# Routed attention with a gated convolution FFN: slots of a head pair and half a batch's queries, the first batch's heads prepared up front, FFN by half batches

## The chip, the cores and the metric

One core of one Trainium2 chip runs the kernel. The metric is device microseconds for one execution of the whole program, the median of several runs. TensorE (PE in the profile) multiplies matrices and transposes, PEld is its weight load, VectorE is DVE, ScalarE is ACT, GpSimd is POOL, and SyncE (SP) issues most DMAs. Each engine takes its instructions in the order in which the program lists them and waits, at each, for the semaphores that it needs. PSUM has eight banks, all of which this kernel uses.

## The reference, cut to what matters

Four batches, eight heads, 768 tokens, head size 64; the FFN takes d_model 512 to d_ff 1024 and back, with a convolution of three taps along the sequence that makes the gate.

```python
q_assign = argmax(einsum(q_n, c_n))          # 16 clusters per head
k_assign = argmax(einsum(k_n, c_n))
mask = q_assign[:, :, :, None] == k_assign[:, :, None, :]
scores = where(mask, (q @ k.T) / 8, -1e9)
attn = softmax(scores); x = attn @ v         # heads side by side: 4 x 768 x 512

h = maximum(x @ w_in, 0.0)                   # 4 x 768 x 1024
conv = sum over k of conv_w[k] * h shifted by k - 1 along the sequence
out = (h * sigmoid(conv)) @ w_out
```

The mask never appears as a matrix. Every token carries extra rows in the score product, which depend on its cluster number and make the score of two tokens of different clusters so low that its exponential is zero.

## The kernel before

Tokens lie in the order "(p j)": partition p holds tokens 6p to 6p+5. Work is laid out by hand in program order, as a loop over 32 heads (four batches of eight), one head in each turn; a turn is called a slot here. It has six score steps, and each computes 128 keys against all 768 queries in two matmuls of 384 columns (`scores`, L174) into one of two PSUM pairs, which ScalarE exponentiates (L181, 128x768).

Between the score steps of slot t, other heads' and other batches' work is put:

- preparation of head t+2: six transposes of q and k side by side into the banks `tra` and `trb` (L104), their copy by VectorE (L108) and ScalarE (L109), the cast on GpSimd (L114) and two DMAs that carry the halves to `extq` and `extk` (L115, L116), the cast of v (L119), twelve small matmuls against the centroids (`assign`, L123), and the argmax: two VectorE operations (L136, L137), a product on GpSimd (L140), a reduction on VectorE (L149), three small GpSimd operations that make `pack` (L151 to L155). In the next slot `pack` is transposed (L158), copied (L162), and two DMAs carry the bias rows (L163, L164);
- the values of head t-1: 36 matmuls of 65 columns (L188) into the bank `avb`, then normalization (L201, L202), and for each second head the transposes of the pair's output (L212) and the copy to `xT` (L215);
- from slot 9 on, one FFN unit, which is a block of 128 features for all 768 tokens of a batch: four matmuls for each half of the tokens into the bank `fp` (`ffn_in`, L229), relu (L239), two copies on GpSimd that fill the shifted ends (`pads`, L243, L244), three taps on VectorE (L255, L257), tanh (L264) and gate (L276) in the slot after;
- output blocks (128 tokens, eight matmuls over the features, L288), also in `fp`, copied by VectorE (L302) and stored. They can start when all eight units of a batch are gated: slots 17 to 22 and 25 to 30.

SyncE's queue has the loads of q, k and v of head t+4 (L94 to L96), the two DMAs of the cast, the bias rows' DMAs and the stores, in program order. GpSimd also sets constant rows of `extq` and `extk` (`ext_rows`, L308 to L310) at the start and in slots 0 and 1, and issues the weights' DMAs.

Ahead of the loop, heads 0 and 1 are prepared. Behind it the last unit of batch 2, the whole FFN of batch 3 (eight units, `last_in`, `last_gate`, `last_out`) and twelve output blocks are left. There the first tap is ScalarE's (L253) and the gate comes from the sigmoid (L268, L282).

Of the kernel before, what the change touches and what calls it, by code (L numbers as in the profile page):

```python
# [17 lines left out]
def kernel(  # L18
# [15 lines left out]


# [11 lines left out]
    VW = D + 2  # L47

# [5 lines left out]

# [5 lines left out]
    avp = avb[:, 0 : J * VW].rearrange("p (j w) -> p j w", j=J)  # L60
    tra16 = tra.bitcast(F16)
    pkT = trb.bitcast(F16)[0 : 4 * J, 1024 - P : 1024]
    asn = trb[:, 256:448].rearrange("p (j t c) -> p j t c", j=J, t=2)
# [3 lines left out]
    xT = const.tile([P, B, R, S], F16, name="xT")  # L67
# [7 lines left out]
    kscale = const.tile([P, 2, J], F16, name="kscale")  # L75

    NE = 4
    extq_b = [const.tile([P, S], F16, name=f"extq{i}") for i in range(NE)]  # L80
    extk_b = [const.tile([P, S], F16, name=f"extk{i}") for i in range(NE)]
    v16_b = [const.tile([P, J, VW], F16, name=f"v16_{i}") for i in range(NE)]
    NHP = 3
    hpad_b = [const.tile([P, J + 2, P], F16, name=f"hpad{i}") for i in range(NHP)]

    def tok(t, hh):
        return t[hh // H, hh % H].rearrange("(p j) d -> p j d", j=J)
# [3 lines left out]
    def load(hh, kq=nc.sync):  # L91
        qk_t[hh] = rot.tile([P, J, 2, D], F32, name="qk_in", tag="qk_in", bufs=4)
        v_t[hh] = rot.tile([P, J, D], F32, name="v_in", tag="v_in", bufs=4)
        nc.sync.dma_start(qk_t[hh][:, :, 0], tok(q, hh))  # L94
        kq.dma_start(qk_t[hh][:, :, 1], tok(k, hh))
        nc.sync.dma_start(v_t[hh][:], tok(v, hh))  # L96


    qkT, c16, attn, x16, hg_b, packs, asgs = {}, {}, {}, {}, {}, {}, {}

    def transposes(h):
        for j in range(J):
            to = tra[:, P * j : P * (j + 1)] if j < 4 else trb[:, P * (j - 4) : P * (j - 3)]
            nc.tensor.transpose(to, qk_t[h][:, j].rearrange("p a d -> p (a d)"), id128[:])  # L104

    def qkT_copy(h):
        qkT[h] = rot.tile([P, S], F32, name="qkT", tag="qkT", bufs=2)
        nc.vector.tensor_copy(out=qkT[h][:, 0:512], in_=tra[:])  # L108
        nc.scalar.activation(qkT[h][:, 512:S], trb[:, 0:256], AF.Copy)  # L109
        del qk_t[h]  # L110

    def cast_qk(h):
        c = rot.tile([P, S], F16, name="c16", tag="c16", bufs=2)
        nc.gpsimd.tensor_copy(out=c[:], in_=qkT[h][:])  # L114
        nc.sync.dma_start(extq_b[h % NE][64:128, :], c[0:64, :])  # L115
        nc.sync.dma_start(extk_b[h % NE][64:128, :], c[64:128, :])  # L116

    def cast_v(h):
        nc.gpsimd.tensor_copy(out=v16_b[h % NE][:, :, 0:D], in_=v_t.pop(h)[:])  # L119

    def assign(h):
        for j in range(J):
            nc.tensor.matmul(  # L123
                trb[:, 256 + 32 * j : 288 + 32 * j],
# [6 lines left out]
    def arg_a(h):  # L131
# [3 lines left out]
        asgs[h] = val  # L135
        nc.vector.tensor_reduce(out=mx[:], in_=asn, axis=AX.X, op=ALU.max)  # L136
        nc.vector.tensor_tensor(  # L137
            out=eqq[:], in0=asn, in1=mx[:].unsqueeze(3).to_broadcast((P, J, 2, C)), op=ALU.is_equal
        )
        nc.gpsimd.tensor_tensor(  # L140
# [3 lines left out]
    def arg_b(h):  # L144
        m_t = rot.tile([P, J, 2], F32, name="m_t", tag="m_t")
        pack = rot.tile([P, 4, J], F16, name="pack", tag="pack")
        packs[h] = pack
        del qkT[h]
        nc.vector.tensor_reduce(out=m_t[:], in_=asgs.pop(h)[:], axis=AX.X, op=ALU.max)  # L149

        nc.gpsimd.tensor_scalar(  # L151
            out=pack[:, 1:3, :], in0=m_t.rearrange("p j t -> p t j"), scalar1=-8.5, scalar2=None, op0=ALU.add
        )
        nc.gpsimd.tensor_tensor(out=pack[:, 0:4:3, :], in0=pack[:, 1:3, :], in1=pack[:, 1:3, :], op=ALU.mult)
        nc.gpsimd.tensor_tensor(out=pack[:, 2:4, :], in0=pack[:, 2:4, :], in1=kscale[:], op=ALU.mult)  # L155

    def pack_transpose(h):
        nc.tensor.transpose(pkT, packs.pop(h).rearrange("p a j -> p (a j)"), id16[:])  # L158

    def bias_rows(h):  # L160
        spk = rot.tile([P, P], F16, name="spk", tag="spk")
        nc.vector.tensor_copy(out=spk[0 : 4 * J, :], in_=pkT)  # L162
        nc.sync.dma_start(extq_b[h % NE][0:2, :], spk[0 : 2 * J, :])  # L163
        nc.sync.dma_start(extk_b[h % NE][1:3, :], spk[2 * J : 4 * J, :])  # L164
# [3 lines left out]
    def scores(h, kt):  # L168
        if kt == 0:
            attn[h] = rot.tile([P, J, S], F16, name="attn", tag="attn", bufs=2)  # L170
        s = sc[nsc[0] % 2]
        nsc[0] += 1
        for half in range(2):
            nc.tensor.matmul(  # L174
                s[:, half, 0:HS],
                lhsT=extk_b[h % NE][:, P * kt : P * (kt + 1)],
                rhs=extq_b[h % NE][:, HS * half : HS * (half + 1)],
# [3 lines left out]
        nc.scalar.activation(  # L181
            attn[h][:, kt, :].rearrange("p (a c) -> p a c", a=2), s[:, :, 0:HS], AF.Exp, scale=0.125
        )

    def values(h, jqs):
        for jq in jqs:
            for kt in range(J):
                nc.tensor.matmul(  # L188
                    avp[:, jq, 0 : D + 1],
                    lhsT=attn[h][:, kt, P * jq : P * (jq + 1)],  # L190
                    rhs=v16_b[h % NE][:, kt, 0 : D + 1],
# [5 lines left out]
    def normalize(h):  # L197
        rec = rot.tile([P, J, 1], F32, name="rec", tag="rec")
        if h % 2 == 0:
            x16[h // 2] = rot.tile([P, J, P], F16, name="x16", tag="x16")  # L200
        nc.vector.reciprocal(out=rec[:], in_=avp[:, :, D : D + 1])  # L201
        nc.vector.tensor_tensor(  # L202
            out=x16[h // 2][:, :, D * (h % 2) : D * (h % 2 + 1)],
            in0=avp[:, :, 0:D],
# [189 lines left out]
    for t in range(NH):  # L394
# [9 lines left out]
        if t + 4 < NH:  # L404
            load(t + 4)
# [135 lines left out]
```

## Time and profile before

| what | us |
|---|---|
| median of 3 runs | 337.9 (337.27 to 339.41) |
| the profiled execution's span | 337.4 |
| first scores of slot 0 / 5 / 9 / 26 | 18.48 / 63.54 / 90.29 / 231.86 |
| end of the last score step | 280.81 |
| VectorE busy | 206.0 (61%) |
| ScalarE busy | 224.5 (67%) |
| GpSimd busy | 139.1 (41%) |
| exponentials: 192 of 0.81 | 151.6 |
| multiply-add taps: 64 of 1.03 | 65.9 |
| `extq`/`extk` constant rows: 12 of 0.73 | 8.7 |

The span is that of one profiled execution. A group's row gives the number of instructions, their busy time and mean duration, and the idle time of the engine ahead of them with the one that ended it. Matmuls overlap in TensorE's pipeline, so that the time from one start to the next, not the duration, tells what a matmul costs its queue. TensorE's granted clock (PEclk) is 1.00 at full speed.

### The profile page before, as it was taken

To read this page: it belongs to the slowest core of one execution; us is meant where nothing else is said; L and a number is where in the kernel's file an instruction comes from. 1 tells how busy PE (TensorE), PEld (TensorE's weight loads), DVE (VectorE), ACT (ScalarE), POOL (GpSimd) and SP (SyncE) were. 2 spreads that over 40 slices of the span, in tenths; PEclk is the share of its full clock that TensorE was granted. 3 is DMA by queue.
4 is the path that set the end of the run, shared out by engine and by line. 5 is a ranking of instruction groups with operands and counts; after the bars stand their busy time and mean duration, and the time that the engine had idled before them with its cause. 6 is when DMAs were issued, how large, how long until landed. Compare 5 with 4: busy or idle time off the path is not lost.

```text
span 337.4 us, 7211 instructions
## 1 busy us (share of the span) xinstructions
PE 283.8 (84%) x2721; PEld 198.4 (59%) x2721; DVE 206.0 (61%) x390; ACT 224.5 (67%) x339; POOL 139.1 (41%) x304
## 2 busy tenths in 40 slices
PE   7585969687989898989999999899999987699762
PEld 7463747566666666667666666666667654345320
DVE  3212424343467776868777778678878668646632
ACT  2143838567777787878777777787777785855532
POOL 3366464445544545455535454545454301110200
PEclk9855989999999999999999999999999999999877
DMA  7138475666733333434244444542431100021005
GB/s 199 39 96 190 104 130 141 130 159 139 182 98 96 94 97 96 105 94 111 75 132 119 126 115 123 142 104 74 129 101 55 58 33 1 31 95 62 0 0 187
DMA packets 66744, 34.26 MB, mean 102 GB/s; under 512 B 53395, under 2 KB 63635, under 8 KB 66710
## 3 DMA queue, kind: packets, MB, share of 16 engines
q1 hardware_dynamic: 63622, 31.51, 34.2%
q0 software_dynamic: 2304, 2.10, 4.3%
q8 instruction: 21, 0.34, 0.5%
q10 hardware_dynamic: 784, 0.20, 0.3%
q14 instruction: 13, 0.11, 0.1%
HBM read 23.11 MB, written 6.29 MB: 87 GB/s over the span
## 4 chain that ended last, share of the span: by engine, by line
PE 53%; ACT 23%; issue 8%; DVE 5%; POOL 5%; DMA 3%; SPq 2%; ACTq 0%; POOLq 0%; DVEq 0%
ACT attn L181 14%; PE trb L123 11%; PE sc L174 11%; PE fp L229 7%; PE avb L188 6%; PE fp L288 6%; PE sc L288 4%; ACT th L264 3%; ACT hpad L239 3%; ACT qkT L109 2%; PE sc L327 2%; DVE cnv L257 2%; PE tra L212 1%; DMA extk<-spk 1%; PE avb L229 1%
## 5 line engine op out<-in xcount | busy, mean ns | idle before, releaser
L181 ACT ACTIVATE attn<-sc 128x768 f16<-128x768 f32 x192 | 151.6, 810 | 72.9 <-PE sc L174 72.5
L174 PE MATMUL sc<-extq,extk 128*128 128x384 f16 x384 | 93.2, 334 | 24.1 <-ACT attn L181 11.6
L257 DVE SCALAR_TENSOR_TENSOR cnv<-hpad,cwcol,cnv 128x768 f16<-128x768 f16 x64 | 65.9, 1031 | 14.8 <-ACT cnv L253 12.9
L140 POOL TENSOR_TENSOR val<-eqq,iota_rev 128x192 f32<-128x192 f32 x32 | 26.6, 830 | 73.5 <-DVE eqq L137 73.5
L174 PEld LDWEIGHTS <-extk 128*128 128x128 f16 x384 | 30.8, 103 | 39.8 <-issue 16.0
L188 PE MATMUL avb<-v,attn 128*128 128x65 f16 x1152 | 53.3, 196 | 0.1
L188 PEld LDWEIGHTS <-attn 128*128 128x128 f16 x1152 | 47.6, 99 | 7.6 <-issue 0.3
L123 PEld LDWEIGHTS trb<-cT,qkT 128*128 128x128 f32 x384 | 48.8, 198 | 3.2 <-ACT qkT L109 1.0
L123 PE MATMUL trb<-cT,qkT 128*128 128x32 f32 x384 | 47.5, 275 | 0.8 <-DVE qkT L108 0.8
L229 PE MATMUL fp<-xT,w_in 128*128 128x384 f16 x224 | 46.2, 329 | 2.0 <-ACT hpad L239 0.7
L229 PEld LDWEIGHTS <-w_in 128*128 128x128 f16 x256 | 25.1, 99 | 26.4 <-issue 11.3
L243 POOL COPY hpad<-hpad 128x127 f16<-128x127 f16 x32 | 10.2, 319 | 66.9 <-ACT hpad L239 66.9
L288 PEld LDWEIGHTS <-hg 128*128 128x128 f16 x192 | 19.3, 101 | 29.3 <-DVE hg L282 6.2
L276 DVE SCALAR_TENSOR_TENSOR hg<-th,hpad 128x768 f16<-128x768 f32 x24 | 28.2, 1173 | 10.5 <-ACT th L264 10.4
L108 DVE COPY qkT<-tra 128x512 f32<-128x512 f32 x32 | 21.8, 682 | 18.5 <-PE tra L104 18.5
L114 POOL CAST c<-qkT 128x768 f16<-128x768 f32 x32 | 26.4, 825 | 14.8 <-DVE qkT L108 8.7
L239 ACT ACTIVATE hpad<-fp 128x384 f16<-128x384 f32 x56 | 27.6, 493 | 2.9 <-PE fp L229 1.8
L201 DVE RECIPROCAL rec<-avb 128x6 f32<-128x6 f32 x32 | 6.3, 196 | 34.6 <-PE avb L188 34.6
L119 POOL CAST v<-v_in 128x384 f16<-128x384 f32 x32 | 27.1, 848 | 0.0
L288 PE MATMUL fp<-w_out,hg 128*128 128x512 f16 x96 | 24.6, 379 | 0.0
L288 PE MATMUL sc<-w_out,hg 128*128 128x512 f16 x64 | 17.7, 413 | 7.2 <-DVE hg L282 5.3
L264 ACT ACTIVATE th<-cnv 128x768 f32<-128x768 f16 x24 | 20.3, 845 | 4.0 <-DVE cnv L257 4.0
(71 smaller groups left out, 303.4 us busy)
## 6 DMA issues: line engine op xcount, KB each, us to landing
qk_in<-in_q_dram SPq DMA_DIRECT2D x32, 192.0 KB
v_in<-in_v_dram SPq DMA_DIRECT2D x32, 192.0 KB
out_dram<-o_sb SPq DMA_DIRECT2D x24, 256.0 KB
qk_in<-in_k_dram SPq DMA_DIRECT2D x31, 192.0 KB
extq<-c SPq DMA_DIRECT2D x32, 96.0 KB
extk<-c SPq DMA_DIRECT2D x32, 96.0 KB
w_in<-in_moe_w_in_dram POOLq DMA_DIRECT2D x8, 128.0 KB, 4.2
w_out<-in_moe_w_out_dram POOLq DMA_DIRECT2D x8, 128.0 KB, 4.5
```

The lines of the kernel that those rows point to most:

```text
L119: nc.gpsimd.tensor_copy(out=v16_b[h % NE][:, :, 0:D], in_=v_t.pop(h)[:])
L123: nc.tensor.matmul(trb[:, 256 + 32 * j : 288 + 32 * j], lhsT=qkT[h][:, P * j : P * (j + 1)], rhs=cT32[:, h % H, :], start=True, stop=True,)
L140: nc.gpsimd.tensor_tensor(out=val[:], in0=eqq[:], in1=iota_rev[:].unsqueeze(1).unsqueeze(1).to_broadcast((P, J, 2, C)), op=ALU.mult)
L174: nc.tensor.matmul(s[:, half, 0:HS], lhsT=extk_b[h % NE][:, P * kt : P * (kt + 1)], rhs=extq_b[h % NE][:, HS * half : HS * (half + 1)], st ...
L181: nc.scalar.activation(attn[h][:, kt, :].rearrange("p (a c) -> p a c", a=2), s[:, :, 0:HS], AF.Exp, scale=0.125)
L188: nc.tensor.matmul(avp[:, jq, 0 : D + 1], lhsT=attn[h][:, kt, P * jq : P * (jq + 1)], rhs=v16_b[h % NE][:, kt, 0 : D + 1], start=(kt == 0) ...
L229: nc.tensor.matmul(bank[:, 0:HS], lhsT=w_in16[:, r, fb, :], rhs=xT[:, b, r, HS * half : HS * (half + 1)], start=(r == 0), stop=(r == R - 1 ...
L239: nc.scalar.activation(flat(hpad(b, fb)[:, 1 + 3 * half : 4 + 3 * half, :]), bank[:, 0:HS], AF.Relu)
L257: nc.vector.scalar_tensor_tensor(out=cnv[:], in0=src, scalar=w, in1=cnv[:], op0=ALU.mult, op1=ALU.add)
L264: nc.scalar.activation(th_t[b, fb][:], cnv_t.pop((b, fb))[:], AF.Tanh, scale=0.5)
L276: nc.vector.scalar_tensor_tensor(out=hg(b, fb), in0=th_t.pop((b, fb))[:], scalar=1.0, in1=flat(hpad(b, fb)[:, 1 : J + 1, :]), op0=ALU.add, ...
L288: nc.tensor.matmul(bank[:, 0:Dm], lhsT=hg_b[b][:, fb, P * sb : P * (sb + 1)], rhs=w_out16[:, fb, :], start=(fb == 0), stop=(fb == NFB - 1) ...
```

## The change

A slot is now a pair of heads with half of a batch's queries: slots 8b to 8b+3 take the four pairs of batch b for the first 384 queries, 8b+4 to 8b+7 for the other 384. There are 32 slots as before. A score step takes two blocks of 128 keys against 384 queries, so that its matmuls and its exponential have the old sizes. Queries are in sequence order; keys and values keep the order "(p j)". `extq` and `extk` have 67 rows instead of 128, without constant filler rows (the constant rows come with `pack`), and there are twelve of each instead of four.

Preparation of a head is done earlier and kept: heads 0 to 2 are begun ahead of the loop, heads 3 to 5 stand in slot 0, heads 6 and 7 in slot 1, and head h in slot h-6 from head 8 on. For heads 0 and 1 the argmax is VectorE's alone. Loads of q and k are eight heads ahead in the loop, over six buffers instead of four.

An FFN unit is two feature blocks for half of a batch's tokens: the first half gates tokens 0 to 381, the second half the other 386, and a small copy on GpSimd (`carry`) hands three columns from one to the other in place of `pads`. A half can start when its four slots are done, so that the FFN runs from slot 5 on, one unit in each slot, with five units behind the loop. A unit has six taps of 382 or 386 columns in place of three of 768. x is transposed in every slot (three blocks) in place of every other (six). Seventeen output blocks stand in the loop, in slots 8b+9, 8b+10 and 8b+13 to 8b+16. Behind the loop the plain tap is GpSimd's.

```diff
-    def tok(t, hh):
-        return t[hh // H, hh % H].rearrange("(p j) d -> p j d", j=J)
+    def load_qk(hh, kq=nc.sync):
+        qk_t[hh] = rot.tile([P, J, 2, D], F32, name="qk_in", tag="qk_in", bufs=6)
+        nc.sync.dma_start(qk_t[hh][:, :, 0], q[hh // H, hh % H].rearrange("(j p) d -> p j d", p=P))
+        kq.dma_start(qk_t[hh][:, :, 1], k[hh // H, hh % H].rearrange("(p j) d -> p j d", j=J))
...
+    def slot(t):
+        b, a, pr = t // SPB, t % SPB // NPR, t % NPR
+        return b, a, pr, b * H + 2 * pr
...
-        for half in range(2):
+        kt = 2 * (g % 3)
+        for i in range(2):
             nc.tensor.matmul(
-                s[:, half, 0:HS],
-                lhsT=extk_b[h % NE][:, P * kt : P * (kt + 1)],
-                rhs=extq_b[h % NE][:, HS * half : HS * (half + 1)],
+                s[:, i, 0:HS],
+                lhsT=extk_b[h % NE][0:KC, P * (kt + i) : P * (kt + i + 1)],
+                rhs=extq_b[h % NE][0:KC, HS * a : HS * (a + 1)],
...
+    def carry(n):
+        b, a, u = unit(n)
+        if a == 0:
+            if u == 0:
+                hfs[b] = rot.tile([P, NFB, 4], F16, name="hf", tag="hf")
+            nc.gpsimd.tensor_copy(out=hfs[b][:, 2 * u : 2 * u + 2, 0:3], in_=hpad(n)[:, :, HS - 1 : HS + 2])
+        else:
+            nc.gpsimd.tensor_copy(out=hpad(n)[:, :, 1:4], in_=hfs[b][:, 2 * u : 2 * u + 2, 0:3])
+    def tap(n, f, i, eng=None):
+        b, a, u = unit(n)
+        N = NCV[a]
...
+        src, cnv = hpad(n)[:, f, 1 + i : 1 + i + N], cnv_t[n][:, f, 0:N]
...
+    at(0, 0, lambda: arg_b(2), lambda: cast_v(2))
+    at(0, 1, lambda: bias_rows(2))
+    prepare(3, 0, 0, 1, 2, 0, 4)
+    prepare(4, 0, 2, 3, 4, 1, 0)
+    prepare(5, 0, 4, 5, 5, 1, 1)
+    prepare(6, 1, 1, 2, 3, 1, 5)
+    prepare(7, 1, 3, 4, 5, 2, 0)
+    for h in range(H, NH):
+        prepare(h, h - 6, 0, 3, 4, h - 5, 1)
+
+    fouts = {}
+    for b in range(B):
+        for tq, t in zip(range(6), (9, 10, 13, 14, 15, 16)):
+            fouts[SPB * b + t] = (b, tq)
+    LAG = NPR + 1
...
     scores(t, 0)
-        if t + 4 < NH:
-            load(t + 4)
...
+        if t < 2:
+            for h in (6 + 2 * t, 7 + 2 * t):
+                load_qk(h)
+                load_v(h)
+        elif t + 8 < NH:
+            load_qk(t + 8)
+            load_v(t + 8)
...
+    last_in(n0)
+    last_in(n0 + 1)
+    for i, (b, tq) in enumerate(whole):
+        bank = (tra, trb)[i % 2]
+        ffn_out(b, tq, range(NFB), bank)
+        evac(b, tq, bank, 0.5, on_act=(i % 2 == 0))
+    for u in range(NPR):
+        sigmoid(n0 + u)
+        gate_sg(n0 + u)
+        if u + 2 < NPR:
+            last_in(n0 + u + 2)
+        last_out(u)
+    for tq in range(2, J):
+        evac(bl, tq, banks[tq - 2], oscale[:] if tq == 2 else 1.0, on_act=(tq % 2 == 0))
```

`prepare(h, t, p0, p1, p2, t3, p3)` puts the transposes, copies and casts of head h behind score step p0 of slot t, assign and the first half of the argmax behind p1, the second half behind p2, and the bias rows behind score step p3 of slot t3.

## The prediction, as it was recorded

> **What bounds the kernel now.** I read the page first, then the busy times by stage, then the chain of waits inside one slot, then VectorE's timeline in the tail. A slot is one turn of the main loop (six score steps); slot 18 below is 163.52 to 172.37 us. From the page: span, TensorE's share, small DMA packets, the chain's shares.
>
> ```profile
> span 337.4 us, 7211 instructions
> ...
> DMA packets 66744, 34.26 MB, mean 102 GB/s; under 512 B 53395, under 2 KB 63635, under 8 KB 66710
> ...
> PE 53%; ACT 23%; issue 8%; DVE 5%; POOL 5%; DMA 3%; SPq 2%; ACTq 0%; POOLq 0%; DVEq 0%
> ```
>
> By stage: start to the first scores; slots 0 to 4; 5 to 8 (no FFN yet); 9 to 16 (FFN without output blocks); 17 to 25; slot 18 alone; 26 to 31; the tail.
>
> ```profile
> core 0: us, PE busy (x) PEld busy (x) DVE busy (x) ACT busy (x) POOL busy (x), PEclk, DMA share, GB/s
> 0.00:18.48 18.48, 11.25 (x63) 10.26 (x64) 5.75 (x20) 3.74 (x6) 7.93 (x24) 0.87 0.43 109
> 18.48:63.54 45.06, 34.40 (x321) 26.20 (x320) 13.87 (x36) 24.82 (x35) 24.91 (x61) 0.79 0.58 130
> 63.54:90.29 26.75, 22.41 (x282) 17.66 (x281) 11.83 (x30) 19.41 (x28) 12.98 (x29) 1.00 0.73 160
> 90.29:155.00 64.71, 55.89 (x626) 41.84 (x624) 47.38 (x90) 50.25 (x80) 31.63 (x64) 1.00 0.40 101
> 155.00:231.86 76.86, 74.15 (x757) 52.56 (x756) 60.03 (x110) 59.53 (x91) 37.27 (x73) 1.00 0.42 114
> 163.52:172.37 8.85, 8.78 (x91) 6.21 (x90) 7.25 (x14) 6.62 (x10) 3.97 (x9) 1.00 0.41 120
> 231.86:280.81 48.95, 46.53 (x474) 31.49 (x473) 36.22 (x66) 38.26 (x58) 18.42 (x40) 1.00 0.25 75
> 280.81:337.40 56.59, 39.20 (x209) 18.36 (x207) 30.97 (x40) 28.46 (x44) 5.95 (x18) 0.88 0.15 56
> ```
>
> TensorE has no idle time in slot 18 (8.78 of 8.85), a quarter idle in slots 0 to 4, and nearly a third in the 56.6 us of tail, where no other engine is full either. The chain in slot 18 (start, us, what) gives TensorE's price per piece, start to start:
>
> ```profile
> 166.81 0.81 PE fp L229 x4
> 167.62 0.38 PE avb L188 x12
> 168.00 0.33 PE sc L174 x2
> 168.32 1.26 PE trb L123 x12
> 169.58 0.34 PE tra L212 x6
> 169.92 0.33 PE sc L174 x2
> 170.24 0.86 PE fp L288 x4
> ```
>
> In the tail each FFN unit crosses engines: VectorE waits for ScalarE's tap, TensorE for the gate.
>
> ```profile
> 310.60 0.55 DVE L282 TENSOR_TENSOR hg<-sg,hpad 128x768 f16<-128x768 f16 x1
> 313.72 2.14 DVE L257 SCALAR_TENSOR_TENSOR cnv<-hpad,cwcol,cnv 128x768 f16<-128x768 f16 x2 [2.58 <-ACT cnv L253]
> 315.78 0.64 DVE L282 TENSOR_TENSOR hg<-sg,hpad 128x768 f16<-128x768 f16 x1
> ```
>
> **What moves.** One half-batch unit (two feature blocks, 382 or 386 tokens) is as much FFN as one old unit (one block, 768 tokens). Of 32 units, 23 lay in the loop and 9 in the tail; now 27 and 5. Of 24 output blocks, 12 and 12; now 17 and 7. FFN starts in slot 5, not 9. Preparing a head stood once in each of slots 0 to 29; now three heads in slot 0, two in slot 1, one in each of 2 to 25, none from 26 on. I sum four stages; the old ends are 63.54, 231.86, 280.81, 337.4.
>
> **Start and slots 0 to 4 (63.5 before).** Head 0's chain gets shorter: its bias rows are copied at 15.31, because assign(1) stood in front on TensorE (13.03 to 15.2), and now they go out about 2.5 earlier. But before the first scores stand head 1's chain on VectorE (three rows of 0.35, the product at 0.36, three small ones near 0.2: 2.0), head 2's copy (0.69) and assign(2) (2.2, as assign(1) took at the half clock): first scores at 18.2 as before, ends 17 and 20. Then SyncE's queue. Its loads are spaced 0.68 (21.02, 21.67, 22.36 on L94 to L96). Between head 2's two DMAs and head 3's stand 14 loads: 9.5. Head 2's leave near 18.7, loads are through at 28.2, head 3's pair and head 2's bias rows (0.6, 0.6, 0.7, 0.7) at 30.8. Old bias rows issued at 16.40 let scores start at 18.24, so add 1.84: slot 1 starts at 32.6, against 30.2. Behind this wait stands all of TensorE's slot 1. Slot 1 prepares two heads through one PSUM bank (transposes 0.65, copy 0.69, assign 1.26, two reductions 0.75, pack 0.3: near 3.7 each), and the cast of head 5 must wait for head 3's DMA, as that tile has two buffers: I take 9.3. Slot 2 is 6.7 (the mean of old slots 5 to 8, 26.75/4) plus 1.2 for a late pack of head 7; slots 3 and 4 are 6.7 each. That is 63.2. GpSimd's row memsets vanish (twelve of 0.73 from the start to slot 1, some on the chain), which these stages without stalls already contain. I take 64; ends 60 (slot 1 on time) and 69 (each stall doubled).
>
> The granted clock was 0.79 over slots 0 to 4. I keep it, since the trace shows it low although TensorE was busy three quarters of that time. The Trainium skill (TensorE: Matmul & The Clock Gate, Part 1) has the clock halved only after an idle window of some 3.4 us and restored by one busy window. By that rule the denser start would keep the clock and an estimate of this stage would be 61, the total 320; the row speaks for less.
>
> Queries now load in sequence order, 256-byte rows at a stride. The tile interleaves q with k, so the 64 q and k loads were 768 pieces of 256 B each already: 49,152 of the 53,395 small packets. I charge nothing; ends nothing and, where a q load took twice its 0.68, four of the 14 loads in that queue, 2.7 us. The Trainium skill (DMA: Bandwidth & Descriptors, Specifications) wants 512 B for line rate, which speaks against this order; its estimate is that upper end.
>
> **Slots 5 to 25 (168.3 before).** TensorE's full slot: six score pairs 1.98, values 1.24, preparation 0.65 + 0.16 + 1.26, FFN-in 1.30, output 1.72, x-transposes 0.17: 8.48, measured 8.68 (mean of 8.85 and 8.52, with and without x-transposes, which every slot now has half of). VectorE: its six taps are half as wide. A 768-wide multiply-add is 1.03, a 384-wide product 0.56, a 192-wide one 0.36: 0.6 each, four make 2.4 against 2.06. The plain tap is 0.41; halves lie between 0.21 and 0.41, I take 0.3: 0.6 against 0.41. xT copies 0.35 each slot against 0.55 every other. Together +0.6 on 7.3, so 7.9. The cover is TensorE's 8.68. What stands at its edge is the bank fp: FFN-in of the next slot waits for VectorE's output copy, which ended at 173.21 for a start at 173.81. Of these 0.6 some 0.45 go. So 8.8 for a full slot; ends 8.52 and 9.3. Pads (two GpSimd copies of 0.3 between relu and tap) become one small copy off that path; a gain, counted nothing. A slot without output: 8.71 and 7.52 before; ScalarE's sum is 6 x 0.81 + 0.38 + 0.85 + 2 x 0.49 = 7.07, and the longer ones wait 1.02 for GpSimd's pack, which comes later behind wider taps: 8.2, ends 7.5 and 8.7. 13 full slots (9, 10, 13 to 18, 21 to 25) and 8 others: 114.4 + 65.6 = 180; ends 171 and 190.5.
>
> **Slots 26 to 31 (49.0 before).** No preparation: TensorE 8.48 - 2.07 = 6.41, ScalarE 7.07 - 0.38 = 6.69, and the output copy is now late by about 0.5. Old slot 30 (no preparation, output) took 8.05, slot 31 (neither) 6.16. I take 4 x 7.4 + 2 x 6.7 = 43; ends 39 and 46.
>
> **Tail (56.6 before).** Old: gates from 295.64 to 325.82, seven steps, 4.31 each. Four units fewer at that price: 39.4, the upper end; five ninths of all of it, 31.4, the lower. By steps: up to the leftover unit's gate 8.4 before (280.81 to 289.23), now 11, since the first FFN-in waits for slot 31's output block (0.86) and copy (0.68), and taps are longer. Then two units' taps (2.6 each), the output copies and the sigmoid table (1.28), sigmoid 0.83, gate 0.55, waits: 9.4; two more units' taps and three gates: 7.8. After the last gate 11.05 before, with 12 matmuls and six copies over four buffers (the last waited 2.2 for a DMA); now 8 and four: 7.5. Sum 35.7.
>
> **Sum.** 64 + 180 + 43 + 35.7 = 322.7 on the profile's 337.4; the median of the runs, 337.9, lies 0.5 above it: 323.
>
> **Rivals.** (1) Slower: VectorE becomes the bound of the loop, at the copy that frees fp. For it: in slot 18 it also stood still 0.85 for the values and 0.4 for the tanh; if such waits stay, 7.9 + 1.25, and gates stretched as one was from 1.0 to 1.34 beside GpSimd, make 9.5. Price: 21 x 9.5 = 199.5 for 180, total 342.5. It decides from a mean slot of 9.4 on. Against it: those waits are slack that TensorE's pace leaves, and slots without output have no such copy. (2) The queue of loads never catches up: slots 1 to 4 each start as late as slot 1, 4 x 2.5 more, and the tail takes 39.4: 337, no change. Against it: from slot 2 on one head is loaded per slot (4.9 us of SyncE's issue for a slot over 6.5) six slots ahead. (3) Better: full clock at the start (61), slots at TensorE's measured 8.68 and 7.9 (176), tail 33: 313. (4) The change does not do what it says: FFN cannot start in slot 5. Against it: slot 4 copies the last pair's xT and slot 5's matmuls stand behind it; price 4 units back in the tail, 4 x 4.31 less what the loop saves (some 7): 333.
>
> **Numbers.** Forecast (316 to 330) 0.61, (3) 0.15, (2) with (4) 0.14, half of it below 334.5, (1) 0.10 of which 0.09 slower. What a measurement can tell from no change is about 1%, 334.5 to 341.3. Faster 0.84, same 0.07, slower 0.09. Range 310 to 335, which leaves out the lower tail of (3), half of the no-change cases and (1); all stages at one end would give 301 or 345.
>
> **What would show it.** Right: first scores of slot 5 near 64, slot 26 near 244, last scores near 287, VectorE's share up from 61% to near 67%, the tail 36 with five gates. Wrong: FFN-in waiting for the output copy in most slots with VectorE without idle time (rival 1); scores waiting for bias-row DMAs beyond slot 2 (rival 2); a clock of 1.00 through slot 1 (rival 3).

## The result, and the profile after

The changed kernel takes 350.35 us, the median of four executions of which three lie at 349.18 to 351.14, against 337.89: the ratio is 1.036, interval 1.031 to 1.041. It is slower by 12.5 us where 15 us less had been forecast. A kernel's median here and below is over all its executions; a ratio, to the kernel before on the same chip, leaves out executions more than 1.5% above the kernel's fastest.

From the page of the profiled execution (349.18 us, span 347.4), the lines that answer to those of before:

```profile
span 347.4 us, 7331 instructions
...
DMA packets 67194, 34.37 MB, mean 99 GB/s; under 512 B 53843, under 2 KB 64083, under 8 KB 67158
...
DVE 41%; PE 40%; issue 8%; ACT 7%; POOL 2%; DVEq 0%; POOLq 0%; ACTq 0%
```

The small packets are as many as before, so that the order of the queries did nothing to their number. In the chain that ended last VectorE has gone from 5% to 41%: it now ends waits that TensorE used to end by itself. By stage: start to first scores; slots 0 and 1; slots 2 to 4; 5 to 25; slot 6 alone; slot 16 alone (a full one); 26 to 31; the tail.

```profile
core 0: us, PE busy (x) PEld busy (x) DVE busy (x) ACT busy (x) POOL busy (x), PEclk, DMA share, GB/s
0.00:17.25 17.25, 13.30 (x82) 12.25 (x82) 8.30 (x30) 4.33 (x8) 4.67 (x32) 0.83 0.57 140
17.25:50.71 33.46, 31.44 (x159) 24.56 (x160) 11.11 (x29) 11.27 (x17) 15.35 (x43) 0.50 0.67 164
50.71:73.73 23.02, 20.86 (x219) 16.20 (x219) 9.29 (x26) 14.82 (x22) 11.13 (x25) 0.82 0.65 142
73.73:261.92 188.19, 170.34 (x1742) 120.95 (x1742) 148.18 (x325) 136.78 (x210) 73.55 (x156) 0.99 0.41 106
81.20:90.37 9.17, 7.07 (x78) 5.19 (x78) 6.90 (x17) 6.48 (x11) 4.48 (x9) 1.00 0.51 117
172.74:181.59 8.85, 8.64 (x87) 6.04 (x86) 7.32 (x17) 6.52 (x11) 3.30 (x7) 1.00 0.43 121
261.92:308.43 46.51, 36.77 (x385) 21.81 (x384) 32.18 (x66) 36.78 (x54) 2.41 (x9) 1.00 0.07 24
308.43:347.40 38.97, 23.50 (x140) 11.03 (x137) 23.07 (x38) 13.87 (x22) 12.60 (x13) 0.94 0.14 55
```

| stage | before | forecast | after | after less forecast |
|---|---|---|---|---|
| start and slots 0 to 4 | 63.5 | 64 | 73.7 | +9.7 |
| slots 5 to 25 | 168.3 | 180 | 188.2 | +8.2 |
| slots 26 to 31 | 49.0 | 43 | 46.5 | +3.5 |
| tail | 56.6 | 35.7 | 39.0 | +3.3 |

The work moved as forecast: the tail gives 17.6 us back, the loop takes them. But each of the four terms came out too small, and together they miss by 24.7. Four readings say where.

**Slots 0 and 1** take 17.3 and 16.2 us at a granted clock of 0.50 while TensorE is busy for 31.44 of 33.46 us. TensorE's timeline in slot 0 (start, duration, instructions), head 4's assign, a score pair, the transpose of head 3's bias rows and four of head 5's six transposes:

```profile
26.05 2.74 PE L134 MATMUL trb<-cT,qkT 128*128 128x32 f32 x12
28.60 0.83 PE L189 MATMUL sc<-extq,extk 67*128 67x384 f16 x2
29.69 0.26 PE L168 MATMUL trb<-id,pack 128*36 128x128 f16 x1 [0.27 <-DVE eqq L148]
29.89 1.12 PE L110 MATMUL tra<-id,qk_in 128*128 128x128 f32 x4
```

The twelve assign matmuls cost 2.55 us to the next start where slot 18 of before paid 1.26, the transposes and the score pair some double as well.

**Slots 6 to 9, 12, 13, 20, 21** are 1 to 1.4 us longer than their neighbours. VectorE, GpSimd and TensorE in slot 6, one fence for each timeline:

```profile
80.89 0.36 DVE L148 TENSOR_TENSOR eqq<-trb,mx 128x192 f32<-128x192 f32 x1
...
81.43 0.61 DVE L275 TENSOR_SCALAR cnv<-hpad,cwcol 128x382 f16<-128x382 f16 x1
82.08 1.27 DVE L277 SCALAR_TENSOR_TENSOR cnv<-hpad,cwcol,cnv 128x382 f16<-128x382 f16 x2
83.26 0.35 DVE L159 TENSOR_REDUCE m_t<-val 128x12 f32<-128x192 f32 x1
```

```profile
81.33 0.59 POOL L151 TENSOR_TENSOR val<-eqq,iota_rev 128x192 f32<-128x192 f32 x1 [2.65 <-DVE eqq L148]
83.77 0.23 POOL L160 TENSOR_SCALAR pack<-m_t 128x12 f16<-128x12 f32 x1 [1.85 <-DVE m_t L159]
```

```profile
85.33 0.23 PE L168 MATMUL trb<-id,pack 128*36 128x128 f16 x1 [1.53 <-ACT hpad L256]
```

GpSimd's product was done at 81.92, but the reduction that reads it (m_t) stands behind three taps in VectorE's queue, starts at 83.26, and pack, its transpose and everything behind it on TensorE come as much later: TensorE stands for 1.53 us. The line names a relu as releaser, since it ended a hundredth or two after pack's last part (85.28); the transpose reads pack. But the relu too comes late through VectorE: it stands behind the tanh of the unit before, which waits for the same three taps (tanh from 83.38, an exponential, relu to 85.3). Which of the two counts is for e2 to tell.

**Slots 26 to 31 and the tail** are shown with their experiments.

### The profile page after: what moved, and what is told of

Its sections match the earlier page's. It is cut to its first block, busy times and chain, and to the rows that moved or that the text cites. A ratio compares the mean times of both kernels' runs of the same rounds, so it can differ in the third digit from the quotient of the medians.

```text
span 347.4 us, 7331 instructions
## 1 busy us (share of the span) xinstructions
PE 296.2 (85%) x2721; PEld 206.8 (60%) x2721; DVE 232.1 (67%) x512; ACT 217.8 (63%) x330; POOL 119.7 (34%) x276
## 2 busy tenths in 40 slices
DMA packets 67194, 34.37 MB, mean 99 GB/s; under 512 B 53843, under 2 KB 64083, under 8 KB 67158
## 4 chain that ended last, share of the span: by engine, by line
DVE 41%; PE 40%; issue 8%; ACT 7%; POOL 2%; DVEq 0%; POOLq 0%; ACTq 0%
DVE cnv L277 18%; PE fp L245 10%; PE avb L203 8%; PE sc L189 6%; DVE cnv L275 6%; PE trb L134 6%; ACT attn L196 3%; DVE o_sb L326 3%; DVE eqq L148 3%; DVE x L216 3%; PE tra L110 2%; ACT th L293 2%; DVE mx L147 2%; DVE xT L230 2%; PE trb L168 2%
## 5 line engine op out<-in xcount | busy, mean ns | idle before, releaser
L189 PE MATMUL sc<-extq,extk 67*128 67x384 f16 x384 | 97.5, 342 | 6.9 <-ACT attn L196 6.9
L277 DVE SCALAR_TENSOR_TENSOR cnv<-hpad,cwcol,cnv 128x382 f16<-128x382 f16 (+1 forms) x128 | 80.7, 633 | 6.9 <-POOL cnv L275 2.7
L151 POOL TENSOR_TENSOR val<-eqq,iota_rev 128x192 f32<-128x192 f32 x30 | 17.7, 589 | 86.3 <-DVE eqq L148 86.3
L189 PEld LDWEIGHTS <-extk 67*128 67x128 f16 x384 | 31.6, 103 | 20.6 <-issue 10.0
L121 POOL CAST c<-qkT 128x768 f16<-128x768 f32 x32 | 33.6, 1051 | 17.4 <-DVE qkT L115 9.4
L312 PE MATMUL fp<-w_out,hg 128*128 128x512 f16 x136 | 34.9, 378 | 0.0
L297 DVE SCALAR_TENSOR_TENSOR hg<-th,hpad 128x764 f16<-128x764 f32 (+1 forms) x28 | 26.7, 954 | 5.8 <-ACT th L293 5.3
L293 ACT ACTIVATE th<-cnv 128x764 f32<-128x764 f16 (+1 forms) x28 | 23.6, 842 | 8.0 <-DVE cnv L277 8.0
L275 DVE TENSOR_SCALAR cnv<-hpad,cwcol 128x382 f16<-128x382 f16 (+1 forms) x56 | 23.8, 425 | 0.0
L147 DVE TENSOR_REDUCE mx<-trb 128x12 f32<-128x192 f32 x30 | 10.6, 353 | 18.1 <-PE trb L134 18.1
L110 PE MATMUL tra<-id,qk_in 128*128 128x128 f32 x120 | 22.1, 315 | 0.0
```

What stands on the lines that cost most here:

```text
L189: nc.tensor.matmul(s[:, i, 0:HS], lhsT=extk_b[h % NE][0:KC, P * (kt + i) : P * (kt + i + 1)], rhs=extq_b[h % NE][0:KC, HS * a : HS * (a + 1)],
L275: (eng or nc.vector).tensor_scalar(out=cnv, in0=src, scalar1=w, scalar2=None, op0=ALU.mult)
L277: nc.vector.scalar_tensor_tensor(out=cnv, in0=src, scalar=w, in1=cnv, op0=ALU.mult, op1=ALU.add)
L293: nc.scalar.activation(th_t[n][:, :, 0:N], cnv_t.pop(n)[:, :, 0:N], AF.Tanh, scale=0.5)
L312: nc.tensor.matmul(bank[:, 0:Dm], lhsT=hg_b[b][:, fb, P * tq : P * (tq + 1)], rhs=w_out16[:, fb, :], start=(fb == 0), stop=(fb == NFB - 1) ...
```

## The experiments

The prediction's reasons and their rivals were taken up stage by stage. "Before" is the kernel before, run on the same chip with the kernels of one group.

### The start: the clock, the loads, the crowding

**Dummy matmuls (e1_fill; e1b_fill_start_only has those ahead of the loop alone).** Their output goes to banks that nobody reads before they are written again.

```diff
+    def fill(bank, k):
+        for _ in range(k):
+            nc.tensor.matmul(bank, lhsT=id16[:], rhs=ones[:], start=True, stop=True)
...
+    fill(sc[1][:, 0, :], 10)
     bias_rows(0)
...
+    fill(sc[1][:, 0, :], 6)
     bias_rows(1)
+    fill(sc[1][:, 0, :], 3)
     assign(2)
...
     def run(t, place):
+        if t < 2:
+            fill((avb if t == 0 else fp)[:], 3)
```

> Dummy matmuls (128x512, their result is never read) are added: 19 in the waits ahead of the loop and 3 at each of the 12 places of slots 0 and 1. Theory 1, the half clock: slots 0 and 1 take 17.3 and 16.2 us because TensorE runs them at half clock, and no stretch of 3.4 us there streams enough columns to lift it. Then the clock stays at or returns to 1.00 before 30 us, slots 0 and 1 fall to 12-15 and 8-11, slot 5 starts at 62-66 instead of 73.7, and the time falls by 7 to 11 us, to 339-343. Rival, loads and the shared PSUM bank: slots 0 and 1 are set by SyncE's queue of loads and by the bank that the head preparations share, and the clock is low because TensorE waits. Then the added work changes nothing or costs up to 5 us: 350-356.

> Only the 19 dummy matmuls ahead of the loop. Theory 1 with the fall of the clock at 11.4 us as its cause: the clock does not fall ahead of slot 0, and falls only if slot 0 itself has too little to stream; slots 0 and 1 lose 4 to 15 us together, time 339-346. If preparation itself (weight loads in fp32 for 32 columns) keeps the streaming share low, the clock falls again inside slot 0 and the gain is at most 3 us, 347-350. Rival (loads and bank): 349-352.

e1_fill: 348.38 us against 336.2 for before (341.87 to 349.06). In the profiled execution (348.47) the clock stayed at 1.00 to 24.5 and came back at 34.7; slot 1 fell from 16.2 to 13.0, but slot 0 rose to 18.7, and slot 5 started at 73.0. e1b: 351.83 (ratio 1.044, 1.037 to 1.050); the clock fell at 22.2, within slot 0, and stayed at 0.50 to 56.3. What took the clock's place in slot 0 of e1_fill is in its chain:

```profile
18.73 0.53 SPq L123
...
19.30 0.59 SPq L124
...
21.05 0.43 SPq L97
...
21.53 3.86 DMA qk_in<-in_k_dram
...
25.43 1.12 PE tra L111 x4
```

SyncE's queue has the casts' DMAs of head 2 (L123, L124) ahead of the loads of v and of head 4 (L97); these land at 25.39, and TensorE stands 1.44 us for them, up to head 4's transposes; the half clock begins within this wait. So the next run moves the loads.

**The loads up, with and without the dummies (e5_fill_loads, e14_loads_only).**

```diff
     load_qk(3)
+    load_qk(4)
...
     cast_qk(0)
+    load_qk(5)
+    load_v(2)
+    load_v(3)
...
-    load_v(2)
-    load_v(3)
-    load_qk(4)
-    load_qk(5)
```

> As e1_fill, and the loads of q, k of heads 4 and 5 and v of heads 2 and 3 are issued some 10 us earlier, in gaps of SyncE's queue between 7 and 14 us. Theory (with the clock up, SyncE's queue of loads is what holds slot 0: heads 4 and 5 arrive at 25.4): slot 0 falls from 18.7 to 12 to 14 us, slot 5 starts at 66 to 69 instead of 73, the whole 341 to 345 against e1's 348.4. Rival (the chain transposes, copy, assign, maximum, pack through the one pair of banks sets slots 0 and 1): slot 0 stays at 17 or more, 347 to 349.

> The early loads of e5 without the dummy matmuls. Theory (half clock first, loads second: the queue holds slot 0 only once the clock is up): 349 to 351 as the change itself, the clock low from 11 to 56. Rival (the loads alone are the cause): slot 0 at 13 to 14, 345 to 347.

e5: 342.02 us (ratio 1.014, 1.009 to 1.020), slot 0 13.0, slot 1 13.0, slot 5 at 63.69. e14: ratio 1.038 (1.031 to 1.045), slots 0 and 1 17.29 and 16.18 to the hundredth as in the change, clock 0.50 from 12.2 to 56.5. The square is complete: loads alone give nothing, dummies alone 2 us at the median, both 8.3, and the start is back at the forecast's 64. But one of e1's four executions, at 341.87 with a mean clock of 0.973, came out as e5's do. The other three, 348.3 to 349.1, had 0.959 to 0.965; in the profiled one of them the 10.24 us at half clock lower the mean by 0.015, about the whole gap to 0.973. So the half clock is the cause with and without the late loads. Their share seems to be that TensorE's wait for them lets the half clock back in; what they would cost at full clock no profile here shows. The window from 11.4 to 55.8 us, first in the change, then in e5:

```profile
11.40:55.80 44.40, 40.07 (x209) 31.32 (x210) 15.36 (x43) 13.38 (x21) 19.30 (x51) 0.50 0.57 135
```

```profile
11.40:55.80 44.40, 40.81 (x363) 29.07 (x361) 19.31 (x56) 20.12 (x30) 23.16 (x59) 1.00 0.69 160
```

TensorE is busy for 90 and 92% of both, at a clock of 0.50 and of 1.00. Busy time is not what decides.

**The same dummies with 64 columns instead of 512 (e15_short_fill).**

```diff
-            nc.tensor.matmul(bank, lhsT=id16[:], rhs=ones[:], start=True, stop=True)
+            nc.tensor.matmul(bank[:, 0:64], lhsT=id16[:], rhs=ones[:, 0:64], start=True, stop=True)
```

> e5_fill_loads with the same 55 dummy matmuls, each over 64 columns instead of 512. If the granted clock follows the columns that are streamed, the clock is low from about 11 to 50 or later as in the change, 348 to 351. If it follows how much of the time TensorE has instructions, or how many, the clock stays up as in e5, 340 to 343.

354.21 us (ratio 1.048, 1.041 to 1.055): no faster than the change, and 3 us above what was expected (in its profile slot 20, with half clock from 214.4 to 224.7, takes 12.1 instead of 9.2). Its stretch from 13.0 to 47.2:

```profile
13.00:47.20 34.20, 32.36 (x192) 27.02 (x191) 12.01 (x34) 10.03 (x15) 14.66 (x41) 0.50 0.57 142
```

Busy for 95%, and half clock for 34 us. So here the clock follows the columns that stream through the array, not how many matmuls there are or how long TensorE counts as busy. Assign is a likely reason why slots 0 and 1 stream so little: twelve matmuls of 32 columns, each with a 128x128 weight load, five times in two slots, some 13 of their 33.5 us. Columns can be counted (512 of f16 in 0.217 us at full clock by e5's dummies, f32 twice that, by the six transposes of 128 columns in 0.65 us in slot 18 of before). The stretch at half clock, 44.37 us, is thirteen windows of 3.41 us, the shortest stretch at one clock that the traces show within a run. The first twelve of the change's hold 0.19 to 0.41 of the full rate, the last 0.46; e5's up to 43 us hold 0.52 to 0.82. The count alone proves little, since a window at half clock can hold no more than 0.5, and whether transposes count like other matmuls was not run; the argument rests on e15. Nor is it a sharp rule: in e15 windows of 0.42 did not lift the clock and one of 0.41 did.

**The kernel before with dummies (e11_before_fill)**, at the same kinds of places.

> The kernel before with dummy matmuls at the start (19 ahead of the loop, 3 ahead of each of the twelve score steps of slots 0 and 1; they write banks that nobody reads). It shows whether the half clock cost the kernel before anything. Its half clock lay from 13.95 to 34.43. Theory (the kernel before waited for loads and bias rows in these slots, so the clock was cheap there): 0 to 3 us gained, 334 to 338. Rival (half clock costs it as much as the changed kernel): slots 0 and 1 fall from 19.6 to 13 to 14, 330 to 333.

339.74 us (ratio 1.008, 1.005 to 1.011): no gain, rather a loss. Slots 0 and 1 took 11.1 and 10.2 instead of 11.7 and 7.9. Before, the first scores of these two slots stood 3.0 and 3.6 us for DMAs of bias rows, and with the dummies still 1.5 and 2.5. So there half clock was cheap, at most what the dummies cost; the two were not separated. The granted clock of 0.79 in the stage of before could therefore not tell what half clock would cost in a stage full of preparation.

**The five early heads spread (e6_spread, e8_spread_ontime).** e6 shifts all later heads by one slot too:

```diff
-    prepare(4, 0, 2, 3, 4, 1, 0)
-    prepare(5, 0, 4, 5, 5, 1, 1)
-    prepare(6, 1, 1, 2, 3, 1, 5)
-    prepare(7, 1, 3, 4, 5, 2, 0)
+    prepare(4, 1, 0, 1, 2, 1, 4)
+    prepare(5, 1, 3, 4, 5, 2, 0)
+    prepare(6, 2, 1, 2, 3, 2, 5)
+    prepare(7, 2, 4, 5, 5, 3, 0)
...
-        prepare(h, h - 6, 0, 3, 4, h - 5, 1)
+        prepare(h, h - 5, 1 if h == H else 0, 3, 4, h - 4, 1 if h < NH - 1 else 0)
```

> Heads are prepared one in slot 0 (3), two in slot 1 (4, 5), two in slot 2 (6, 7), then one per slot up to slot 26, instead of three and two and one up to slot 25; nothing else. Theory (five preparations crowded into two slots at half clock, each at a double price of some 4 us): slots 0 to 2 take 34 to 37 instead of 42.6 us, slot 5 starts at 66 to 69 and the whole is 343 to 347 against 350.3; slot 26 gets back at most 1.5. Rival (the half clock alone is the price and is lifted no sooner, so work moved is work paid later): slot 5 starts at 72 or later, 349 to 351.

376.02 us (ratio 1.113, 1.105 to 1.120): a clear miss for both theories. Its chain in slot 11:

```profile
153.41 0.43 SPq L171
...
153.89 1.86 DMA extk<-spk
...
155.80 0.82 PE sc L189 x2
```

Pair 3 of a batch is wanted four slots into its batch (head 15 in slot 11), so with preparation one slot later its bias rows land after the scores that need them: slots 11 and 19 took 14.1 and 13.6 instead of 7.9, and slot 5 began at 90.2. e8 keeps everything in time (heads 3, 4 in slot 0, 5, 6 in 1, 7 in 2, the others as in the change) on top of e5:

```diff
-    prepare(4, 0, 2, 3, 4, 1, 0)
-    prepare(5, 0, 4, 5, 5, 1, 1)
-    prepare(6, 1, 1, 2, 3, 1, 5)
-    prepare(7, 1, 3, 4, 5, 2, 0)
+    prepare(4, 0, 3, 4, 5, 1, 0)
+    prepare(5, 1, 0, 1, 2, 1, 4)
+    prepare(6, 1, 3, 4, 5, 2, 0)
+    prepare(7, 2, 1, 2, 3, 2, 5)
```

> As e5_fill_loads (clock kept up, loads early), with the five early heads spread 3, 4 | 5, 6 | 7 over slots 0 to 2, each still in time for its first scores; heads 8 on as in the change. In e5 slots 0, 1, 2 took 13.0, 13.0, 7.6. Theory (each preparation is a chain of some 4 us through one pair of banks, so a slot cannot be shorter than its heads times that): 8.5 to 9 each for two heads, slot 5 at 56 to 59 instead of 63.7, the whole 335 to 338 against e5's 342. Rival (the late bias rows, as in e6, or the loads set these slots): slots 1 to 3 stretch by a late DMA and the sum stays at 33 or more, 341 to 345.

345.88 us (ratio 1.028, 1.021 to 1.035), slower than e5. Slots 0 to 2 take 11.2, 14.1, 10.5, in sum 35.9 against 33.6. Slot 0 gains, slots 1 and 2 lose, and slots 3 and 4, partly at half clock (59.2 to 66.0), take 8.4 and 8.3 instead of 6.2. GpSimd's timeline in slot 1:

```profile
33.42 1.32 POOL L430 DMA_DIRECT2D w_in<-in_moe_w_in_dram  x2 [2.52 <-issue]
34.74 0.84 POOL L122 CAST c<-qkT 128x768 f16<-128x768 f32 x1
35.51 0.51 POOL L127 CAST v<-v_in 128x384 f16<-128x384 f32 x1
35.98 0.59 POOL L152 TENSOR_TENSOR val<-eqq,iota_rev 128x192 f32<-128x192 f32 x1
```

Head 5's cast, whose source VectorE had copied by 31.9, stands behind the issue of the weights' DMAs (program order puts those at the end of slot 0, and the cast now behind them), and its product stands behind the casts. Whether this is all of it wasn't separated. Nor does e8 show that crowding costs anything: e5, with the five heads in two slots, is faster.

### Slots 5 to 25: a reduction behind taps

```diff
-            taps(n, 1)
+            tap(n, 1, 1)
         run(t, 4)
+        if n is not None:
+            tap(n, 1, 0)
+            tap(n, 1, 2)
```

> The second half of the argmax (a reduction on VectorE, three small GpSimd operations) is put between the first and the second of the three taps of the slot's second feature block, instead of behind all three. Theory 2: slots 6 to 9, 12, 13, 20 and 21 take 9.2 and 10.2 instead of the 8.2 and 8.8 forecast because TensorE's transpose of pack waits 1.5 us for this chain. Then these slots fall by about 1.0 to 1.3 each, the time by 7 to 10: 340-343. Rival: VectorE's work bounds these slots, and the wait only moves to the tanh and the output copy: change within 2 us.

344.04 us (ratio 1.023, 1.017 to 1.028), 6.3 less than the change by the medians, 4.6 by the ratios, where 7 to 10 had been expected. In the profile slots 5 to 25 take 182.3 instead of 188.2. In slot 6:

```profile
81.44 0.62 DVE L275 TENSOR_SCALAR cnv<-hpad,cwcol 128x382 f16<-128x382 f16 x1
81.98 0.34 DVE L159 TENSOR_REDUCE m_t<-val 128x12 f32<-128x192 f32 x1
82.24 1.25 DVE L277 SCALAR_TENSOR_TENSOR cnv<-hpad,cwcol,cnv 128x382 f16<-128x382 f16 x2
```

m_t starts 1.28 earlier, pack's transpose at 83.90 instead of 85.33, and TensorE's next wait in the slot is the one behind it:

```profile
85.50 0.81 PE L245 MATMUL fp<-xT,w_in 128*128 128x384 f16 x4 [0.56 <-ACT hpad L256]
```

So pack was the wait, and the relu behind the tanh is the next, 0.56 us long. Slots 6, 8, 12 fall from 9.2 to 8.45, slots 9, 13, 21 from 10.2 to 9.46, full ones from 8.85 to 8.72. (Slots 7 and 20 held a window of half clock in this run, 9.2 and 9.1.) Slots 9, 13 and 21 stay long: the first full slots after slots without output, with VectorE busy for 8.2 of 9.46 us.

### Slots 26 to 31: one bank for three things

TensorE's waits ahead of FFN-in in the change from 261 us on (in total, times, the longest), the first ended by the relu of a unit's first half, the second by the output copy:

```profile
PE fp L245 <- ACT hpad L256: 3.5, 5, 1.2
PE fp L245 <- DVE o_sb L326: 2.6, 5, 1.2
```

The relu's are 1.19 in slots 28 and 29 and 0.37 in 27, 30 and 31; the copy's 0.88 in slot 26, 0.2 in 27, 30 and 31, and 1.21 behind the loop.

**The output block in another bank (e4_trb_out)**, from slot 26 on.

```diff
+            bank = trb if t > 25 else fp
-            ffn_out(*fout, range(0, 4), fp)
+            ffn_out(*fout, range(0, 4), bank)
...
-            evac(*fout, fp, 0.5)
+            evac(*fout, bank, 0.5)
```

> The output blocks of slots 26 to 31 go to the bank trb, which no head uses from there on, instead of fp. Theory (the two input halves of a unit and the output block share the bank fp, so each first ffn_in waits for the output copy): slots 26, 29, 30, 31 and the tail's first ffn_in each lose the wait of some 1.2 us, the six slots take 42 instead of 46.5 us, the whole 345 to 346.5 against 350.3. Rival (VectorE's order of work sets these slots: 24 taps of 0.6, copies, normalising): the wait only moves from the bank to the taps, less than 1 us is gained, 349.5 to 350.5.

348.95 us (ratio 1.037, 1.031 to 1.043), slots 29 to 31 to the hundredth as before the edit: 8.38, 7.89, 7.19. Behind the loop the wait of 1.21 is gone, and the tail takes 37.7 instead of 39.0. In the slots the output copy was the releaser that the chain named, but not the only thing in the way. The chain of e4 in slot 30:

```profile
295.95 0.50 ACT th L293
...
296.57 0.80 ACT attn L196
297.38 0.39 ACT hpad L256
...
297.81 0.81 PE fp L245 x4
```

The second half's ffn_in waits for the relu of the first half, which shares its bank, and this stands behind the tanh and an exponential on ScalarE. e9 and e10 test it, both with e8's start and e2's order; e10 moves the second half, with the output block, out of the first half's bank from slot 27 on:

```diff
-            ffn_in(n, 1, fp)
-            relu(n, 1, fp)
+            late = trb if t > 26 else fp
+            ffn_in(n, 1, late)
+            relu(n, 1, late)
...
-            evac(*fout, fp, 0.5)
+            evac(*fout, late, 0.5)
```

> e8 with e2's edit (m_t and pack of the head between the first and the second tap). The two lie in different slots, so e2's 6 us come off e8 whole: e8 less 6 to 6.5. If not, less than 4, one of the gains covered the other.

> e9, and from slot 27 on the second input half of a unit and the output block go to the bank trb. e4 moved the output alone and slots 29 to 31 stayed at 8.38, 7.89, 7.19: its chain has the second ffn_in wait for the first half's relu, which is queued behind an exp and the tanh on ScalarE. Theory (that is the wait that took the place of the output copy): slots 27 to 31 take 34 to 35.5 instead of 37.7, the whole 2.5 to 4 below e9. Rival (VectorE's taps set these slots): under 1 us.

e9: 340.65 us (ratio 1.006, 1.002 to 1.011), 5.2 below e8. e10: 334.91 (ratio 0.993, 0.990 to 0.997), 5.7 below e9 by the medians, 4.4 by the ratios; in the profiles slots 27 to 31 take 34.4 instead of 37.7 (29 to 31: 7.02, 7.03, 6.33) and the tail 37.7 instead of 38.9. In the five slots none of TensorE's waits for the relu is left. The theory holds for them; the tail's part, as in e4, it had not counted. The second half moved alone was not run, so that it may be enough for the slots.

### The tail, and all together

**The plain tap on VectorE (e3_tail_tap):** `taps(n, f)` in place of `taps(n, f, nc.gpsimd)`.

> Behind the loop the plain tap goes from GpSimd (1.26 us each, eight of them, VectorE waits 0.3 to 1.2 for most) to VectorE (0.31). If these waits are on the path: 2 to 4 us less, 346-348. If VectorE's 0.31 only fills other waits: within 1 us.

349.68 us (ratio 1.040); tail 38.5 instead of 39.0, nearly nothing, though GpSimd's tap takes 1.26 where VectorE's takes 0.32: VectorE waits 3.74 us for the first sigmoid instead of 2.63. VectorE in the change's tail:

```profile
326.55 0.69 DVE L326 TENSOR_SCALAR o_sb<-trb 128x512 f32<-128x512 f32 x1
329.86 0.56 DVE L308 TENSOR_TENSOR hg<-sg,hpad 128x772 f16<-128x772 f16 x1 [2.63 <-ACT sg L304]
331.65 3.11 DVE L277 SCALAR_TENSOR_TENSOR cnv<-hpad,cwcol,cnv 128x386 f16<-128x386 f16 x4 [1.23 <-POOL cnv L275]
```

It stands for 2.63 us for the first sigmoid, which is behind ScalarE's copies of whole output blocks and the table load, and on ScalarE the third unit's relus stand behind that sigmoid. e13 changes that order, and gives the second unit's input banks of its own; e12 is the same without it (the start of e5, the order of e2, the bank of e10).

```diff
+    last_in(n0, (avb, fp))
     taps(n, 0)
     taps(n, 1)
+    last_in(n0 + 1, (tra, trb))
     tanh(n)
+    gate(n - 1)
+    last_taps(n0)
     gate(n)
+    last_in(n0 + 2, (avb, fp))
+    sigmoid(n0)
+    last_taps(n0 + 1)
+    gate_sg(n0)
+    whole_out(0, tra, True)
+    whole_out(1, trb, False)
...
```

> The change with the start of e5_fill_loads (dummy matmuls, early loads, heads 3, 4, 5 in slot 0 and 6, 7 in slot 1 as in the change), the order of e2 (m_t between the taps) and the banks of e10 from slot 27 on. If the causes of the start, of slots 5 to 25 and of slots 26 to 31 are separate, the gains add: 342.0 less 6.3 less 4, 331 to 333. If the spread of heads in e8 to e10 had helped after all, 335 or more.

> e12 with the tail's order changed: input halves and relus of the first two last units ahead of the tanh, the whole output blocks and their copies behind the first sigmoids, so that taps follow taps on VectorE. Theory (the tail's units wait in line for ScalarE's copies, table and relus, in the order that the code gives): VectorE's own work from the last values on is near 19 us, so the last gate comes near 26 us after the last scores instead of 31, the tail 33 to 35 instead of 39, the whole 4 to 6 below e12. Rival (GpSimd's plain taps of 1.26 and the table set the pace): under 1.5 us.

e12: 330.62 us (ratio 0.980, 0.974 to 0.985). e13: 326.40 (ratio 0.967, 0.962 to 0.972): faster than both kernels. VectorE in e13's tail, where taps follow taps:

```profile
303.54 2.86 DVE L278 SCALAR_TENSOR_TENSOR cnv<-hpad,cwcol,cnv 128x386 f16<-128x386 f16 x4
306.32 0.55 DVE L309 TENSOR_TENSOR hg<-sg,hpad 128x772 f16<-128x772 f16 x1
306.80 0.68 DVE L327 TENSOR_SCALAR o_sb<-trb 128x512 f32<-128x512 f32 x1
307.40 2.86 DVE L278 SCALAR_TENSOR_TENSOR cnv<-hpad,cwcol,cnv 128x386 f16<-128x386 f16 x4
```

And its four stages:

```profile
0.00:66.23 66.23, 60.28 (x512) 45.66 (x513) 28.97 (x86) 30.12 (x46) 31.25 (x99) 0.95 0.73 168
66.23:248.56 182.33, 172.74 (x1742) 122.12 (x1742) 148.90 (x325) 137.12 (x210) 85.00 (x156) 0.98 0.42 110
248.56:291.18 42.62, 37.19 (x385) 22.70 (x384) 31.98 (x66) 35.91 (x54) 2.57 (x9) 0.96 0.07 26
291.18:325.30 34.12, 23.44 (x140) 10.88 (x137) 22.71 (x38) 13.78 (x22) 12.50 (x13) 0.95 0.17 62
```

66.2, 182.3, 42.6 and 34.1 stand against the forecast's 64, 180, 43 and 35.7. So the profile's 325.3 comes within 3 us of the forecast's 322.7, by another program: the first stage has the dummies' 12 us of added matmuls, the tail an order that the forecast did not have. The forecast had priced the work of the loop about right and left out what stood in its way. In e13's tail order and banks changed together.

**A first try at the sum (e7_all)** had e6's late heads in it:

> The edit of e2 (m_t and pack between the first and the second tap), that of e4 (from slot 27 on), that of e6 and the early loads of e5, without the dummy matmuls. If the causes are separate the gains add: 6.3 + 3.5 + 5 and perhaps 1 from the loads, 334 to 337: the change would then be level with the kernel before. If they share a cause or one wait takes the place of another, 339 to 343. The granted clock in slots 0 to 2 tells whether sparser slots get it back earlier than at 55.8 us.

368.66 us (ratio 1.075, 1.067 to 1.082), with slots 11 and 19 at 13.2 and 13.4 from late bias rows. It could not tell whether the gains add; e12 did.

## Why the prediction was wrong

It called the change faster with a chance of 0.84, at 323 us, range 310 to 335; it was 350.35. (Its cases add up to 0.83 faster and 0.08 same, not 0.84 and 0.07.)

- **Start and slots 0 to 4 (64 forecast, 73.7 measured): the step that failed first.** It priced slot 1 at 9.3 us from "near 3.7 each" for a head, with rows taken at full clock (transposes 0.65, assign 1.26), and kept the granted clock of 0.79 only as a remark. Slot 1 took 16.2 us at 0.50. Slot 0 took 17.3 against 14.4 (18.2 to 32.6). The stage's upper end, 69, doubled the two named stalls but not TensorE's own price. First scores came at 17.25 against 18.2, well sized.
- **The weighing of the Trainium skill (TensorE: Matmul & The Clock Gate, Part 1).** The page has the full clock back after one busy window; in the change TensorE was busy for 90% of thirteen windows in a row, five of them without a gap, at half clock, and e15 shows the columns to matter. The prediction was right to distrust the rule here, but did not carry the row's low clock into the prices.
- **Slots without output (65.6 forecast for eight) and the first full ones.** Eight slots took 69.2, since "GpSimd's pack, which comes later behind wider taps" was sized by slots of before (8.2) and came 1 us later still: it is VectorE's m_t behind three taps, not GpSimd. Slots 9, 13, 21 took 10.2, not 8.8, half of it for the same wait. e2 gives 5.9 of the 8.2 back. Full slots were 8.85 against 8.8, VectorE's share 67% as forecast.
- **Slots 26 to 31 (43, measured 46.5).** "The output copy is now late by about 0.5" named a wait and sized it about right: it was 0.88 in slot 26 and 0.2 in three others. The term that was missing is TensorE's wait for the relu of the first half, in the same bank, behind tanh and an exponential on ScalarE: 1.19 in slots 28 and 29, 0.37 in three others, and as soon as the copy is out of the way (e4) 0.71. e10 removes both.
- **Tail (35.7, measured 39.0).** The steps were right: the leftover unit's gate ended 11.0 us after the last scores, as forecast, but the next one 22.0 after instead of 20.4 (11 + 9.4), and the last 31.3 instead of 28.2. It is the order of copies, table and units on ScalarE and VectorE (e13), not GpSimd's slower tap (e3).
- **Rivals.** (1), VectorE as the bound of the loop at the output copy, did not hold: a mean slot of 8.96 (188.2/21), below its 9.4; VectorE's order, not its load, cost time. (2), the queue of loads, costs nothing at half clock (e14) and, where the clock is up, a wait of 1.44 us in slot 0 (e1). (Its "six slots ahead" is a misreading: head t+8 is loaded in slot t and prepared in slot t+2.) (3) took the clock the wrong way. (4) fell: FFN starts in slot 5.
- **The queries' order** was charged nothing, against the upper end of 2.7 us, an estimate for which the prediction named the Trainium skill (DMA: Bandwidth & Descriptors, Specifications), since pieces stay below its 512 B. By the traces charging nothing was right: there are 53,843 small packets against 53,395, and a q load's issue takes 0.39 us on SyncE's queue (median of 32) where it took 0.60 before, with k loads at 0.62 and 0.65.
- **The range.** Two terms ended beyond their upper ends (73.7 over 69, 46.5 over 46), two just within (188.2 under 190.5, 39.0 under 39.4). The range to 335 took it that their errors would not all go one way, but three of the four left out a wait of the same sort, something short that others wait for, in a queue that had become denser, and the first stage left out its clock.

## What to carry to other kernels

Work that is brought together into few slots may run at another clock than the rows that it is priced from: price it at the clock that such work gets, and look at how many columns it streams, not at how busy TensorE is. When a change doubles the small steps on an engine's queue, go through that queue in program order and ask which short instruction, on which another engine waits, now stands behind long ones. A wait that a chain names may have another right behind it, so that taking it away leaves a slot as long as it was (e4).

## What the runs showed of the hardware

- Half clock for 44 us with TensorE busy for 90%, and full clock throughout with 512-column dummies added (e5): some 12 us of added matmul work, 55 of 0.217, and with the loads moved still 8.3 us faster.
- A plain tap of 382 or 386 columns on VectorE takes 0.31 us, but 0.61 beside GpSimd's product: in the change so do all 21 that ran beside it, and the 34 others took 0.31 or 0.32. In the tail 386 columns take GpSimd 1.26.
- A q load's issue takes SyncE's queue 0.39 us when a partition's six rows of 256 B lie 32 KB apart in memory, and 0.60 when they lie one behind the other.
- Single windows of half clock come at other times in each kernel. In the change one (66.1 to 69.5) makes slot 4 7.75 us where e5 has 6.18, and another (100.2 to 103.6) leaves slot 8 at 9.20 beside 9.17; what brings them in a loop at steady work was not found.
